# Reordering the opening and the first layer-1 stretch of a one-core attention, Fourier and channel-MLP kernel: pads cleared first, a table's halves on ScalarE, a cast in pieces, and new places for the second weights, batch 2's loads and a small state read

## The chip, the cores and the metric

One core of a Trainium2 chip runs the whole program. The metric is the device time of one execution in microseconds (us), lower is better. "Span" is the profiled part of one execution; it is about 1.8 us shorter than its time.

Engines: PE is TensorE's matmul and PEld its weight load, DVE is VectorE, ACT is ScalarE, POOL is GpSimd, SPq is the queue from which SyncE issues DMA transfers. An execution is called slow if it took over 1.5% longer than the fastest of the same kernel. Ratios and intervals come from fast executions only.

## The reference, cut to what matters

```python
# B, H, S, Ns, D = 8, 8, 512, 32, 64
xread = softmax(x @ state.T / 8) @ state         # 512 rows per batch and head
sread = softmax(state @ x.T / 8) @ x             # 32 rows per batch and head
x = concat(xread, sread) -> (8, 576, 512)        # heads side by side
mixed = real(fft(fft(x, axis=1), axis=2))
u = x + mixed
un = (u - mean) / sqrt(var + 1e-6)               # over the last axis
out = u + relu(un @ w_ch1) @ w_ch2               # 512 -> 2048 -> 512
```

The batches are independent of one another. In each, the scores come first, then the reads, then the Fourier sums, then the two layers.

## The kernel before

The kernel works on one batch at a time, and interleaves small steps of the next batch's attention with the large matmuls of this batch's layers. The Fourier transform is done as matmuls against cosine and sine tables, on sums and differences of mirrored rows. The names that matter below:

- `xs` is a batch's x as loaded (f32), `xin` its bf16 copy (the "cast"), `xT` and `sT` are the transposes of x and state, made by DMA. `esp` are the scores.
- `XF` and `XR` are the reads in forward and reversed row order, `Sm` is a sum of the two, `SS`, `XE`, `XO` and `XQ` are the sums for the transform. Their bf16 low parts (`XEl`, `XQl`) are made by GpSimd and are called "low rows" here.
- `gp` is the transform over rows, `G` its copy, `yp` the transform over columns, made with the second table `TEO`. `U` is u.
- `stb` holds the states as bf16. The state in reversed row order is made by two DMAs: `s_dram<-in_state_dram` writes it to memory, `gen<-s_dram` reads it back.
- `ph` and `po` are layers 1 and 2, with the weights `w1` and `w2` (both `w` in the profile). `warm` are matmuls without a result, put in to keep TensorE's clock up. In the recorded texts `over_s` is the first product of `gp`.

Three places in the opening. The pads are cleared behind the first weights' issue, the halves are on VectorE, and the cast is one instruction:

```python
    def second_halves():
        nc.vector.tensor_scalar(TEO[:, :, 1], in0=TEO[:, :, 0], scalar1=sg, ...)
        nc.vector.tensor_scalar(TEO[0:1, 2], in0=TEO[0:1, 2], scalar1=0.5, ...)
    ...
    for q in range(4):
        nc.gpsimd.dma_start(out=w1[:, :, q * 512:(q + 1) * 512], in_=w1v[...])
    constants()
    clears(0)                # its first two memsets are the pads of XF and XR
    ...
    cast_x(1)
```

And the order of work while batch 0's layer 1 runs (`L[i]` are pieces of that layer, `r1[i]` pieces of batch 1's reads):

```python
    state_blocks(2, 3, nc.gpsimd.tensor_copy)
    turned[2, 0]()           # SyncE: transposes of batch 2's state
    make_mirror()
    nc.gpsimd.tensor_tensor(gate, xs_of[0][:, 0:4], w1[:, :, 3 * 512], op=ALU.add)
    load_x(2)                # SyncE: seven loads of batch 2's x
    turn_in_dram(3, B)       # SyncE: the states of batches 3 to 7, rows reversed
    # [... layer 1 and batch 1's scores ...]
    r1[0](); L[6](); r1[2]()
    load_w2()                # GpSimd: waits for batch 2's x, then issues 4 loads
    r1[1](); L[7](); r1[3](); L[8](); r1[4]()
    cast_x(2)                # GpSimd
    turned[2]()              # SyncE: transposes of batch 2's x
    load_state(3, B, s_dram); load_x(3)
    clear_state(3, B)
```

`load_w2` begins with a one-column copy from `xs` of batch 2, the "gate": it keeps the weights from going ahead of batch 2 in the DMA engines.

The softmax here doesn't subtract the row's maximum and nothing guards it: scores larger than these inputs give would overflow.

## Time and profile before

| | before |
|---|---|
| time, median of 3 | 308.58 us (307.76 to 309.93) |
| span of the profiled execution | 306.6 us |
| TensorE busy | 289.3 us, 94% |
| VectorE, ScalarE, GpSimd busy | 184.4, 135.2, 90.5 us |
| first `yp` of batch 0 | 25.01 us |
| first `gp` of batch 1 | 48.27 us |
| first `yp` of batch 1 | 54.54 us |
| first scores of batch 2 | 57.14 us |

The columns are start, duration, engine, line of the kernel, operation, what it writes from what, shapes, how many in a row, and in brackets how long the engine had waited before it and for whom.

```profile
27.01 2.59 SPq L356 DMA_TRANSPOSE sT<-stb  x2
29.78 5.04 SPq L140 DMA_DIRECT2D xs<-in_x_dram  x7
...
38.66 0.18 POOL L304 COPY gate<-xs 128x4 f32<-128x4 f32 x1
38.79 3.03 POOL L306 DMA_DIRECT2D w<-in_moe_w_ch_dram  x4
...
45.34 6.55 SPq L367 DMA_TRANSPOSE xT<-xin  x4
...
48.27 0.24 PE L754 MATMUL gp<-TC,XQ 128*128 128x144 bf16 x1 [1.90 <-DVE XQ L512]
...
54.54 0.27 PE L659 MATMUL yp<-TEO,G 128*128 128x256 bf16 x1
...
57.14 0.40 PE L411 MATMUL esp<-sT,xT 128*128 128x64 bf16 x8
```

Batch 2's x is asked for at 29.78, behind the transposes. It opens GpSimd's gate, behind the gate stand the weights' issues, the low rows and the cast, behind the cast the transposes of x, and behind those the first scores of batch 2 at 57.14. Nobody waits for that chain: the gate shows no wait.

### The profile page before, as it was taken

How to read it: one execution, taken by the hardware profiler on the slowest of the kernel's cores; microseconds unless marked ns; L12 is line 12 of the kernel's file. 1: busy time of each engine (PE TensorE's matmuls, PEld its weight loads, DVE VectorE, ACT ScalarE, POOL GpSimd, SP SyncE). 2: the span in 40 equal slices, each digit the busy share in tenths (PEclk: the TensorE clock that was granted, in tenths of full speed). 3: DMA queues.
4: the chain of work that ended last, by engine and by line, in shares of the span. 5: the costliest groups of instructions: out<-in, count | busy, mean ns of one | idle time of the engine just before them, and what ended most of it. 6: DMA issues, size and time to landing. Idle time of an engine off the chain costs nothing.

```text
span 306.6 us, 5976 instructions
## 1 busy us (share of the span) xinstructions
PE 289.3 (94%) x2280; PEld 166.3 (54%) x2311; DVE 184.4 (60%) x449; ACT 135.2 (44%) x255; POOL 90.5 (30%) x214
## 2 busy tenths in 40 slices
PE   5697997989999999999999999999999999999996
PEld 4576985545544555456644554445444544555443
DVE  6597689858688485782927756684668484100112
ACT  5566773475653535235452545235523442333300
POOL 5783192483154023600307022701340041000000
PEclk9979997999999999999999999999999999999999
DMA  8992989973942955449252594263343034500346
GB/s 154 203 202 46 177 131 182 184 149 60 188 98 62 191 116 137 90 88 223 50 104 87 109 201 98 58 133 75 82 93 68 34 54 103 116 23 34 68 122 154
DMA packets 110794, 34.86 MB, mean 114 GB/s; under 512 B 101950, under 2 KB 106302, under 8 KB 110766
## 3 DMA queue, kind: packets, MB, share of 16 engines
q1 hardware_dynamic: 100046, 28.72, 46.0%
q0 software_dynamic: 4224, 4.19, 8.5%
q10 hardware_dynamic: 6496, 1.57, 2.5%
q8 instruction: 18, 0.29, 0.4%
q14 instruction: 10, 0.08, 0.1%
HBM read 22.41 MB, written 14.02 MB: 119 GB/s over the span
## 4 chain that ended last, share of the span: by engine, by line
PE 83%; DVE 9%; issue 2%; POOL 2%; DMA 2%; ACT 1%; SPq 0%; DVEq 0%; POOLq 0%; ACTq 0%
PE po L959 36%; PE ph L895 34%; PE gp L754 3%; PE ph L905 2%; DMA xs<-in_x_dram 2%; PE yp L659 1%; PE yp L660 1%; PE po L951 1%; PE xrp L436 1%; POOL w L296 1%; DVE Sm L503 1%; PE xfp L436 1%; PE eTp L423 1%; PE esp L411 1%; DVE TEO L268 1%
## 5 line engine op out<-in xcount | busy, mean ns | idle before, releaser
L959 PE MATMUL po<-w,hT 128*128 128x512 bf16 x478 | 122.5, 381 | 1.6 <-issue 0.9
L897 ACT ACTIVATE hT<-ph 128x512 bf16<-128x512 f32 x112 | 66.8, 597 | 118.3 <-PE ph L895 116.3
L895 PE MATMUL ph<-unT,w 128*128 128x512 bf16 x435 | 112.7, 379 | 0.6
L895 PEld LDWEIGHTS <-w 128*128 128x128 bf16 x576 | 50.6, 98 | 47.4 <-issue 0.8
L959 PEld LDWEIGHTS <-hT 128*128 128x128 bf16 x496 | 47.2, 98 | 46.8 <-issue 0.6
L926 DVE SCALAR_TENSOR_TENSOR ot<-po,rstd,U 128x512 f32<-128x512 f32 (+2 forms) x33 | 24.2, 733 | 51.4 <-PE po L959 49.2
L758 POOL COPY GL<-G 128x128 bf16<-128x128 bf16 x7 | 2.0, 289 | 73.2 <-ACT G L755 73.2
L664 DVE TENSOR_TENSOR U<-yp,XR 128x512 f32<-128x512 f32 x14 | 9.6, 683 | 22.9 <-PE yp L660 22.9
L322 POOL TENSOR_TENSOR rstd<-mv,epst 128x1 f32<-128x1 f32 x34 | 6.6, 194 | 52.0 <-DVE mv L318 52.0
L316 DVE BATCH_NORM_STATS2 st<-U 128x6 f32<-128x512 f32 x32 | 21.7, 679 | 0.0
L323 POOL TENSOR_TENSOR rstd<-rstd,mhalf 128x1 f32<-128x1 f32 x34 | 20.1, 590 | 2.7
L755 ACT CAST G<-gp 128x288 bf16<-128x288 f32 x28 | 13.3, 484 | 8.8 <-PE gp L754 8.8
L905 PE MATMUL ph<-unT,w 128*128 128x128 bf16 x256 | 16.5, 221 | 0.3 <-ACT unT L825 0.3
L143 POOL CAST xin<-xs 128x2048 bf16<-128x2048 f32 (+1 forms) x9 | 14.9, 1660 | 2.5 <-DMA xs<-in_x_dram 2.4
L905 PEld LDWEIGHTS <-w 128*128 128x128 bf16 x256 | 15.2, 99 | 0.7 <-issue 0.6
L813 DVE TENSOR_SCALAR ub<-U,mv 128x512 bf16<-128x512 f32 x24 | 12.3, 512 | 0.9
L991 PE MATMUL warm<-ident 128*128 128x128 bf16 x74 | 8.5, 265 | 3.5 <-POOL xs L285 3.5
L907 ACT ACTIVATE hT<-ph 128x512 bf16<-128x512 f32 x16 | 9.3, 595 | 3.8 <-PE ph L905 3.7
L445 DVE TENSOR_TENSOR XR<-xrp,rs 128x512 bf16<-128x512 f32 x14 | 9.7, 694 | 0.6
L487 POOL COPY XT<-XR 32x514 bf16<-32x514 bf16 x6 | 3.6, 602 | 21.8 <-DVE XR L445 21.7
L445 DVE TENSOR_TENSOR XF<-xfp,rs 128x512 bf16<-128x512 f32 x14 | 9.7, 691 | 0.5
L664 DVE TENSOR_TENSOR U<-yp,XF 128x510 f32<-128x510 f32 x14 | 9.5, 676 | 0.0
(231 smaller groups left out, 377.0 us busy)
## 6 DMA issues: line engine op xcount, KB each, us to landing
xs<-in_x_dram SPq DMA_DIRECT2D x22, 256.0 KB, 3.9
w<-in_moe_w_ch_dram POOLq DMA_DIRECT2D x8, 512.0 KB, 10.4
out_dram<-ot SPq DMA_DIRECT2D x15, 256.0 KB, 3.2
r_dram<-ot SPq DMA_DIRECT2D x14, 256.0 KB, 2.6
out_dram<-r_dram SPq DMA_DIRECT2D x14, 256.0 KB, 3.7
xs<-in_x_dram SPq DMA_DIRECT2D x8, 192.0 KB, 5.0
xs<-in_x_dram ACTq DMA_DIRECT2D x2, 256.0 KB, 5.6
l_dram<-ot SPq DMA_DIRECT2D x2, 256.0 KB, 2.2
```

The lines of the kernel that those rows point to most:

```text
L143: copy(xin_bufs[b % 2][:, lo:hi, 1:513], xs_of[b].rearrange("p (i c) -> p i c", i=4)[:, lo:hi])
L316: nc.vector.bn_stats(st6, u)
L323: nc.gpsimd.tensor_tensor(rstd, rstd, mhalf, op=ALU.pow)
L445: nc.vector.tensor_tensor(ov, in0=p[ps, :, 0:256].rearrange("p g (h d) -> p g h d", d=D), in1=rs[ps].unsqueeze(3).to_broadcast([n, 2, 4, D ...
L664: nc.vector.tensor_add(u.rearrange("p (k r) -> p k r", r=2), p.rearrange("p (r k) -> p k r", r=2)[:, 0:u.shape[1] // 2, :], x.rearrange("p ...
L755: nc.scalar.copy(G[:, j, :].rearrange("p (i q) -> p q i", q=2), p[:, 0:NM].rearrange("p (q i) -> p q i", q=2))
L813: nc.vector.tensor_scalar(t, in0=ud, scalar1=mv[:, 0:1], scalar2=None, op0=ALU.subtract)
L895: nc.tensor.matmul(ph[:, o:o + n], lhsT=w1[:, c, f * 128:(f + 1) * 128], rhs=un_of[key][:, c, :], start=(c == 0), stop=(c == DC - 1))
L897: nc.scalar.activation(hT[:, per * i:per * i + per, :].rearrange("p a b -> p (a b)"), ph, AF.Relu, scale=-1.0 / 512 if key == 0 else -1.0 ...
L905: nc.tensor.matmul(ph[:, o:o + 128], lhsT=w1[:, c, f * 128:(f + 1) * 128], rhs=un_of[key][:, c, 128 * r:128 * r + 128], start=(c == 0), st ...
L926: nc.vector.scalar_tensor_tensor(ot[:, cols], in0=po_of[i][:, 0:cols.stop - cols.start], scalar=rstd, in1=u[:, cols], op0=ALU.mult, op1=AL ...
L959: nc.tensor.matmul(po_of[i], lhsT=h_of[key][:, f, i * 128:(i + 1) * 128], rhs=w2[:, f, :], start=(f == 0), stop=(f == FC - 1))
```

## The change

Its intent: take three stalls out of the way (VectorE waiting for the pads; VectorE held up beside GpSimd's cast of batch 1; the same beside the cast of batch 2). The diff, cut to its core:

```diff
     def second_halves():
-        nc.vector.tensor_scalar(TEO[:, :, 1], in0=TEO[:, :, 0], scalar1=sg, scalar2=None, op0=ALU.mult)
-        nc.vector.tensor_scalar(TEO[0:1, 2], in0=TEO[0:1, 2], scalar1=0.5, scalar2=None, op0=ALU.mult)
+        nc.scalar.activation(TEO[:, :, 1], TEO[:, :, 0], AF.Copy, scale=sg)
+        nc.scalar.mul(TEO[0:1, 2], TEO[0:1, 2], 0.5)
 # [...]
     nc.gpsimd.memset(xs_of[1][0:1, 0:1], 0.0)
+    clear_pads(0)
+    clear_pads(1)
 # [...]
+    constants()
+    clears(0)
     for q in range(4):
         nc.gpsimd.dma_start(out=w1[:, :, q * 512:(q + 1) * 512], in_=w1v[:, :, q * 512:(q + 1) * 512])
-    constants()
-    clears(0)
 # [... sread of batches 0 and 1 becomes sread_heads: one product per head into
 #      XQ, and state_rows: four transposing matmuls and one copy into XR ...]
-    cast_x(1)
+    for i in range(4):
+        cast_x(1, lo=i, hi=i + 1)
 # [... second_halves() moves up, behind second_sines(); the warm(10) that stood there becomes warm(6) ...]
-    turned[2, 0]()
     make_mirror()
     nc.gpsimd.tensor_tensor(gate, xs_of[0][:, 0:4], w1[:, :, 3 * 512], op=ALU.add)
     load_x(2)
+    turned[2, 0]()
     turn_in_dram(3, B)
 # [...]
     L[6]()
+    load_w2(0, 2)
     r1[2]()
-    load_w2()
     r1[1]()
-    L[7]()
-    r1[3]()
-    L[8]()
-    r1[4]()
     cast_x(2)
     turned[2]()
     load_state(3, B, s_dram)
     load_x(3)
-    clear_state(3, B)
+    load_w2(2, 4)
+    L[7]()
+    r1[3]()
+    r1[6]()
+    L[8]()
+    r1[4]()
 # [...]
+    clear_state(3, B)
```

`load_w2(lo, hi)` issues the quarters lo to hi - 1 and has the gate only where lo is 0; `r1[6]` is `state_rows`. I call the hunks of the pads, the first weights' issue, the halves (with four warming matmuls fewer) and the cast in pieces the opening, and the rest the tail.

More of the change, by code (lines that the diff above doesn't have):

```diff
@@ L267, in second_halves, with clear_pads, clears @@
     def second_halves():
-        nc.vector.tensor_scalar(TEO[:, :, 1], in0=TEO[:, :, 0], scalar1=sg, scalar2=None, op0=ALU.mult)
-        nc.vector.tensor_scalar(TEO[0:1, 2], in0=TEO[0:1, 2], scalar1=0.5, scalar2=None, op0=ALU.mult)
+        nc.scalar.activation(TEO[:, :, 1], TEO[:, :, 0], AF.Copy, scale=sg)
+        nc.scalar.mul(TEO[0:1, 2], TEO[0:1, 2], 0.5)
     def exp_again():
         nc.scalar.activation(gate2[:, 3:4], gate2[:, 0:1], AF.Exp)
-    def clears(i):
+    def clear_pads(i):
         nc.gpsimd.memset(XFs[i][:, :, 512:514], 0.0)
         nc.gpsimd.memset(XRs[i][:, :, 0:514:513], 0.0)
+    def clears(i):
         if i == 0:
@@ L294, with load_w2 @@
         cast_x(0, lo=i, hi=i + 1)
+    constants()
+    clears(0)
     for q in range(4):
         nc.gpsimd.dma_start(out=w1[:, :, q * 512:(q + 1) * 512], in_=w1v[:, :, q * 512:(q + 1) * 512])
-    constants()
-    clears(0)
     def clear_state(lo, hi):
         nc.gpsimd.memset(stb[:, lo:hi].rearrange("p b g c -> p (b g c)").bitcast(F32), 0.0)
-    def load_w2():
-        nc.gpsimd.tensor_copy(gate, xs_of[2][:, 0:2048:512])
-        for q in range(4):
+    def load_w2(lo, hi):
+        if lo == 0:
+            nc.gpsimd.tensor_copy(gate, xs_of[2][:, 0:2048:512])
+        for q in range(lo, hi):
             nc.gpsimd.dma_start(out=w2[:, q * 4:(q + 1) * 4, :], in_=w2v[:, q * 4:(q + 1) * 4, :])
@@ L447, in xread @@
                 in1=rs[ps].unsqueeze(3).to_broadcast([n, 2, 4, D]), op=ALU.mult)
-        def sread():
-            rcs = wk.tile([128, 2], F32, name="rcs", tag="rcs")
-            for g in range(2):
-                p = qt("srp")
-                for si in range(4):
-                    nc.tensor.matmul(p[:, 0:257], lhsT=E[:, si, g, :], rhs=xin[:, si, 257 * g:257 * g + 257],
-                                     start=(si == 0), stop=(si == 3))
-                nc.vector.reciprocal(rcs[:, g:g + 1], p[:, 256 * g:256 * g + 1])
-                for hh in range(4):
-                    c0 = 512 - (256 * g + 64 * hh)
-                    ph = slice(32 * hh, 32 * hh + 32)
-                    o = XR[0:32, 0, c0:c0 - 64:-1]
-                    i = p[ph, 1 - g + 64 * hh:65 - g + 64 * hh]
-                    if g == 0 and b > 0:
-                        nc.vector.tensor_scalar(o, in0=i, scalar1=rcs[ph, g:g + 1], scalar2=None, op0=ALU.mult)
-                    else:
-                        nc.scalar.activation(o, i, AF.Copy, scale=rcs[ph, g:g + 1])
         def sread_by_head():
@@ L483, in sread_by_head, with sread_heads, state_rows @@
                                         in1=rcs[ph].unsqueeze(2).to_broadcast([32, 2, D]), op=ALU.mult)
+        def sread_heads():
+            p = qt("srp")
+            for g in range(2):
+                for si in range(4):
+                    for hh in range(4):
+                        c0 = 1 + 256 * g + 64 * hh
+                        nc.tensor.matmul(p[32 * hh:32 * hh + 32, 64 * g:64 * g + 64], lhsT=E[:, si, g, 32 * hh:32 * hh + 32],
+                                         rhs=xin[:, si, c0:c0 + 64], start=(si == 0), stop=(si == 3))
+            for g in range(2):
+                for si in range(4):
+                    nc.tensor.matmul(p[:, 128 + g:129 + g], lhsT=E[:, si, g, :], rhs=xin[:, si, 0:1], start=(si == 0), stop=(si == 3))
+            rcs = wk.tile([128, 2], F32, name="rcs", tag="rcs")
+            nc.vector.reciprocal(rcs, p[:, 128:130])
+            nc.vector.tensor_tensor(XQ[:, 0:2 * D].rearrange("p (g d) -> p g d", g=2),
+                                    in0=p[:, 0:128].rearrange("p (g d) -> p g d", g=2),
+                                    in1=rcs.unsqueeze(2).to_broadcast([128, 2, D]), op=ALU.mult)
+        def state_rows():
+            p = qt("hdp")
+            pv = p[0:32, :].rearrange("p (h g d) -> p h g d", h=4, g=2)
+            for hh in range(4):
+                nc.tensor.matmul(pv[:, hh], lhsT=ident[:, 32 * hh:32 * hh + 32], rhs=XQ[:, 0:2 * D].rearrange("p (g d) -> p g d", g=2),
+                                 start=True, stop=True)
+            nc.scalar.copy(XR[0:32, 0, 512:0:-1].rearrange("p (g h d) -> p h g d", g=2, d=D), pv)
         def read_low():
@@ L534, in attend @@
         if b < 2:
-            second = [read_low, sread, fold_low, read(0, False, XF[:, 0, 0:512]),
+            second = [read_low, sread_heads, fold_low, read(0, False, XF[:, 0, 0:512]),
                       lambda: (fold_rows(slice(0, 1)), fold_low_again()),
-                      read(128, False, XF[:, 1, 0:512]), None,
+                      read(128, False, XF[:, 1, 0:512]), state_rows,
                       lambda: (read(256, True, XR[:, 1, 1:513])(), fold())]
@@ L1042 @@
     second_sines()
-    warm(10)
+    second_halves()
+    warm(6)
     even(1)
@@ L1057 @@
     terms_of(2, 0)
-    second_halves()
     out_of(1)
```

## The prediction

> **What bounds the kernel now.** I read the page's slices first, then the waits of the first 50 us, the order of work around each long wait, and the chain that ended last. From the page (40 slices of 7.7 us, busy tenths; PEclk is the granted TensorE clock):
>
> ```profile
> PE   5697997989999999999999999999999999999996
> PEclk9979997999999999999999999999999999999999
> ```
>
> From slice 9 on TensorE is full: cut into stretches, it is busy 9.95 of 10 us in 70:80 and 49.58 of 50 in 200:250. What comes after about 60 us is TensorE work that the change leaves as it is. So a microsecond is worth something only where it lets that stretch begin earlier, and I looked for what delays it. The waits in 0:50 (who, for whom: total us, times, longest):
>
> ```profile
> POOL XEl L490 <- DVE XT L487: 9.6, 1, 9.6
> ...
> DVE XR L604 <- POOL XR L276: 3.1, 1, 3.1
> ...
> PE gp L754 <- DVE XQ L512: 1.9, 1, 1.9
> ...
> PE yp L659 <- DVE G L736: 1.6, 1, 1.6
> ```
>
> GpSimd's 9.6 us is idleness of an engine that nobody waits for there. The other three are on the path, and the order of work shows what is behind each (start us, us, engine, instruction). First, VectorE's first normalisation waits 3.12 us for the clearing of a pad, which stands in GpSimd's queue behind four issues of the first weights:
>
> ```profile
> 9.03 3.20 POOL L296 DMA_DIRECT2D w<-in_moe_w_ch_dram  x4
> ...
> 12.35 0.16 POOL L276 MEMSET XR<- 128x4 bf16 x1
> ...
> 12.54 0.69 DVE L604 TENSOR_TENSOR XR<-xrp,rs 128x512 bf16<-128x512 f32 x1 [3.12 <-POOL XR L276]
> ```
>
> Second, the table's halves on VectorE take 2.59 us beside GpSimd's cast of batch 1, and the copies of G, for which TensorE waits, stand behind them:
>
> ```profile
> 21.20 1.89 POOL L143 CAST xin<-xs 128x2048 bf16<-128x2048 f32 x1
> 21.22 2.59 DVE L268 TENSOR_SCALAR TEO<-TEO,sg 128x512 bf16<-128x512 bf16 x1
> ...
> 23.98 0.88 DVE L736 CAST G<-gp 128x288 bf16<-128x288 f32 x3
> ```
>
> Third, the same with batch 2's cast and the row sum Sm, which takes 0.43 us at 40.17 and 2.70 here:
>
> ```profile
> 42.90 2.70 DVE L503 TENSOR_TENSOR Sm<-XF,XR 128x514 bf16<-128x514 bf16 x1
> 43.40 1.91 POOL L143 CAST xin<-xs 128x2048 bf16<-128x2048 f32 x1
> ```
>
> The chain runs through all of these, and through VectorE, ScalarE and small TensorE steps between 35.9 and 48.2 us; in 28.2 to 35.7 and after about 60 it is TensorE alone.
>
> **What the Trainium skill says.** "SBUF — State Buffer", § Who interferes with whom: VectorE and GpSimd share one pair of ports under an exclusive lock; a tensor_scalar in a two-port mode contends with GpSimd, a tensor_tensor with two SBUF inputs contends with a GpSimd instruction that reads SBUF, and one with at most one SBUF input outside these modes does not. The trace agrees: 2.59 and 2.70 us above, while normalisations out of PSUM keep 0.69 to 0.70 us beside any GpSimd work. "DMA: Bandwidth & Descriptors", § SWDGE vs HWDGE vs iDMA: a DMA from GpSimd has its descriptors computed there; the four issues held GpSimd 3.20 us. "ScalarE: Activation LUTs", § Table sets: copy is in every set, so the halves on ScalarE need no table load; a trace duration for such work is the 0.72 us of a 128x512 activation with a pointer (TEO at 20.23). "TensorE: Matmul & The Clock Gate", § What's actually happening: the clock falls to half after an idle window of some 3.4 us. The trace: after the idle of 46.4 to 48.3 a 128x512 matmul takes 631 ns where 379 is usual, until 52.4; after the idle of 1.6 us at 23.4 there was no such drop.
>
> **The change, part by part (times of the new kernel are estimates from the durations above).**
>
> *Pads first.* Four clears at a pitch of 0.035 us go ahead of GpSimd's casts, where it waited 2.42 us for a DMA anyway. The normalisation starts at 9.45 instead of 12.54. Next in line is the fourth score: it needed VectorE's reciprocal (13.48 + 0.20) and now finds it at about 11.0, but needs ScalarE's copy of x, which ended at 11.40. So it starts at 11.45, not 13.74: 2.3 of the 3.1 us come through. VectorE's normalisations and even/odd sums up to 21.29 follow at that distance. The remaining clears (some 0.8 us) now go ahead of the weights' issue: 9.9 to 13.1; GpSimd's low rows, which started at 15.91, can start at 13.45.
>
> *Halves to ScalarE.* VectorE loses 2.59 + 0.21 us. ScalarE gains about 0.7 + 0.35 after the sines (about 17.2 to 18.2), before its first copy of G (21.67 - 2.3 = 19.3): hidden. The last copies of G then wait for TensorE's last term, which ended at about 22.95, now 20.65; two copies of 0.27 bring 21.2, TensorE goes on at 21.35 where it was 25.01. Shift so far 3.65, of which this part has 1.35: not 2.8, since the terms end behind VectorE anyway. The cast in four pieces (about 18.8 to 21.8; pieces took 0.84 alone) meets only copies out of PSUM, and ends before the transposes of batch 1 (25.88 - 3.65 = 22.2).
>
> *First weights.* They landed at 16.8, 20.2, 22.8 and 25.4; now up to 0.8 later. Layer 1 would start at 24.3 and read a further quarter each 1.3 us, the last at some 28.3: no wait. Batch 2's load waits for the last quarter: about 26.1 instead of 29.78, as two transposes of 2.59 us no longer precede it.
>
> *State read by head.* 32 + 8 + 4 small matmuls (0.46 + 0.29 + 0.22 us of issue) replace 8 of 257 columns (0.86): even. The path from 37.27 to 40.15 (two reciprocals, four multiplies of VectorE, four of ScalarE, 0.28 to 0.32 each) becomes reciprocal, one multiply of 0.29, transposing matmuls and a copy of 0.60, which meet normalisations needed anyway: 0.6 us gained on the path to the first row sum.
>
> *Second weights in two pairs.* GpSimd now waits for batch 2 (26.1 + 8.3, as before from 29.78 to 38.1: 34.4), issues two (1.55), does the low rows (1.4), and casts at about 37.5 to 39.4. The second Sm comes to about 38.8: 0.6 us are still lost there instead of 2.27. Behind it XQl (four of 0.45) may press on XE and XQ: up to 0.5.
>
> *Sum.* From 35.9 on: 3.65 + 0.6 + 2.27 - 0.6 - 0.3 = 5.6 us at the first XQ (48.2 to about 42.6). TensorE has layer-1 work until about 42.1, so its idle time falls from 1.9 to about 0.5 us and I expect the clock to hold: over_s, layer 1 and the first layer-2 products ran some 4 us at about half rate and lost about 1.8. Of that only the 0.89 us that VectorE waits at 55.18 for yp passes on; beyond it VectorE's four statistics (51.0 to 54.3) and the sums of U set the pace. 5.6 + about 0.7 = 6.3, less an allowance of 0.4 for small waits in the new order: 5.9 us. 308.6 - 5.9 = 302.7.
>
> **Rivals.** (1) The lock moves rather than goes: the cast covers the second Sm whole, or GpSimd's low rows hold XE and XQ as three successive GpSimd instructions held Sm at 42.9. For it: the cast is still only 1 us from Sm by my times. Against: batch 2 would have to land later than 35. It makes the shift 4.2 to 4.5, the clock drops again, and the time 304.2. (2) Weights become the bound: the first ones later and needed 3.65 us sooner, or the third and fourth quarter of the second, issued at about 39.5 to 41. They took 5.7 to 13.2 us to land; needed at about 49.5 and 52. For: the queues are full then; against: less traffic stands before them. It costs 1 to 2 us: 304.5. (3) All stalls add up: 3.1 + 2.8 + 2.3 + 0.6, and the clock 1.8. This asks that nothing else is as late, and the fourth score and the last terms are. It would give 299. (4) Hidden altogether, as TensorE is 94% busy: against it, the stalls lie before 60 us and end on the chain, where TensorE's busy time is partly warming matmuls.
>
> **Range and chances.** The uncertain sizes are the contention in 38 to 43 (about 1 us each way), the clock (0.7) and the landing of weights (up to 1.5 one way). I take 300.9 to 304.9. Two per cent is 6.2 us, a little more than I expect: faster by over 2% 0.42, within 2% 0.57, slower 0.01.
>
> **What would show it.** Right: no wait of VectorE for the pads, and the fourth score at about 11.5 behind ScalarE's copy; TEO halves on ScalarE under 0.8 us; first yp at 21.4, layer 1 at 24.3; Sm under 1.2 us; first XQ at about 42.6; no 631 ns matmuls near 44 to 48; from 60 on the same TensorE work, some 6 us earlier. Wrong: layer 1 waiting for w, GpSimd's second gate later than 35.5, Sm or XE near 2 us, po waiting for w2, or a gap of TensorE over 1.5 us with a low clock at about 40 to 46.

## The result, and the profile after

| | before | after |
|---|---|---|
| median of the predicted job | 308.57 us (307.76 to 309.93) | 301.25 us (300.73 to 306.59) |
| ratio of fast runs | 1 | 0.9756, interval 0.9719 to 0.9793 |

A ratio is the mean time of one kernel's fast runs over that of the other's of the same rounds, so it is not quite the ratio of the medians. The change is 7.3 us faster in the median of this job. In two further jobs (after_again and after_five below) the ratio was 0.9821 and 0.9813, with intervals that reach 0.9893 and 0.9854; so the gain is clear, and whether it is over 2% is not.

The four executions after were 306.59, 301.2, 301.3 and 300.73. The first is slow, and it is the one with the profile. A fifth, outside this median, took 301.49. I ran the same kernel in two more jobs, and both times the profiled execution was slow again (307.2 and 308.46). So no profile of a fast execution of exactly this kernel exists. Up to 43 us the three profiles agree closely (the first `gp` of batch 1 starts at 42.92 in this one, at 42.77 and 42.69 in the others), and I read them there. For what follows I use a variant that differs in one place and whose profile is a fast one (`four_first`, below).

The page's slices of after, the rows that answer to those shown in the prediction:

```profile
PE   5989895799999999999999999999999999999996
...
PEclk9999999999999999999999999999999999999999
```

TensorE's clock is never below 90% in a slice. Before, slices 3 and 7 had a 7 there (15.3 to 23.0 us and 46.0 to 53.7 us, at 7.66 us a slice). The 5 and 7 in slices 7 and 8 of the row PE are gaps of this slow execution between 46 and 61 us.

The waits of after in 0:60 (who, for whom: total us, times, longest):

```profile
PE po L969 <- DMA w<-in_moe_w_ch_dram: 3.6, 2, 2.2
...
POOL gate L308 <- DMA xs<-in_x_dram: 2.7, 1, 2.7
...
PE esp L415 <- DMA xT<-xin: 1.7, 2, 1.2
...
PE xrp L440 <- DVE XF L449: 1.5, 1, 1.5
...
PE esp L590 <- ACT xT L578: 0.6, 1, 0.6
```

Gone are VectorE's 3.1 us for the pads, TensorE's 1.9 for `XQ` and 1.6 for `G`. New are GpSimd's wait for batch 2's x at the gate, and TensorE's waits for the second weights (`po`) and for batch 2's transposes (`esp`). For this kernel the last two are known from slow executions only, since no other was profiled. TensorE waits for `xT` in fast executions of variants too (1.5 us in four_again, 0.2 in four_first).

The timeline of after, opening:

```profile
9.47 0.69 DVE L614 TENSOR_TENSOR XR<-xrp,rs 128x512 bf16<-128x512 f32 x1
...
9.74 3.33 POOL L302 DMA_DIRECT2D w<-in_moe_w_ch_dram  x4
...
17.13 0.72 ACT L268 ACTIVATE TEO<-TEO,sg 128x512 bf16<-128x512 bf16 x1
...
18.77 2.29 POOL L143 CAST xin<-xs 128x512 bf16<-128x512 f32 x4
...
20.68 0.27 PE L669 MATMUL yp<-TEO,G 128*128 128x256 bf16 x1 [0.27 <-DVE G L746]
```

The first normalisation starts at 9.47 without a wait (before: 12.54). The table's half costs ScalarE 0.72 us where it cost VectorE 2.59. `yp` of batch 0 starts at 20.68, which is 4.33 us earlier.

The timeline of after, from there to batch 2's first scores:

```profile
22.22 7.18 SPq L140 DMA_DIRECT2D xs<-in_x_dram  x7
29.51 2.68 SPq L360 DMA_TRANSPOSE sT<-stb  x2
...
31.80 0.19 POOL L308 COPY gate<-xs 128x4 f32<-128x4 f32 x1 [2.68 <-DMA xs<-in_x_dram]
...
35.13 1.90 POOL L143 CAST xin<-xs 128x2048 bf16<-128x2048 f32 x1
...
35.32 2.01 DVE L513 TENSOR_TENSOR Sm<-XF,XR 128x514 bf16<-128x514 bf16 x1
...
37.06 15.56 SPq L371 DMA_TRANSPOSE xT<-xin  x4
...
39.63 0.49 DVE L513 TENSOR_TENSOR Sm<-XF,XR 128x514 bf16<-128x514 bf16 x1
...
42.92 0.23 PE L764 MATMUL gp<-TC,XQ 128*128 128x144 bf16 x1
...
55.41 0.29 PE L415 MATMUL esp<-sT,xT 128*128 128x64 bf16 x4 [1.18 <-DMA xT<-xin]
```

Batch 2's x is now asked for at 22.22, 7.56 us earlier, and its transposes of state come behind it. The cast runs at 35.13, beside the first `Sm` (2.01 us; 1.75 and 1.17 in the other two profiles) and no longer beside the second (0.49). `gp` of batch 1 starts 5.35 us earlier and without a wait. The transposes of `xT` take 15.56 us to issue where they took 6.55. Between `gp` and batch 2's first scores TensorE waits 3.6 us for the second weights and 1.2 us for `xT`, and the first scores come only 1.7 us earlier in this execution.

### The profile page after: what moved, and what is told of

Its sections match the earlier page's. It is cut to its first block, busy times and chain, and to the rows that moved or that the text cites. A ratio compares the mean times of both kernels' runs of the same rounds, so it can differ in the third digit from the quotient of the medians.

```text
span 304.8 us, 6036 instructions
## 1 busy us (share of the span) xinstructions
PE 286.5 (94%) x2312; PEld 164.0 (54%) x2343; DVE 181.0 (59%) x443; ACT 135.6 (44%) x254; POOL 91.3 (30%) x217
## 4 chain that ended last, share of the span: by engine, by line
PE 78%; DMA 11%; SPq 4%; POOL 3%; issue 1%; DVE 1%; ACT 1%; ACTq 0%; POOLq 0%; DVEq 0%
PE po L969 35%; PE ph L905 34%; DMA xT<-xin 5%; SPq L140 3%; DMA s_dram<-in_state_dram 3%; DMA xs<-in_x_dram 3%; PE gp L764 2%; PE po L961 1%; PE yp L669 1%; PE yp L670 1%; POOL w L310 1%; PE xfp L440 1%; PE xrp L440 1%; PE esp L415 1%; PE eTp L427 1%
## 5 line engine op out<-in xcount | busy, mean ns | idle before, releaser
L143 POOL CAST xin<-xs 128x512 bf16<-128x512 f32 (+1 forms) x12 | 15.1, 1280 | 2.5 <-DMA xs<-in_x_dram 2.4
L1001 PE MATMUL warm<-ident 128*128 128x128 bf16 x70 | 7.4, 249 | 3.5 <-POOL xs L287 3.5
L420 ACT ACTIVATE E<-esp 128x512 bf16<-128x512 f32 x14 | 8.4, 599 | 2.6 <-PE esp L415 2.6
```

What stands on the lines that cost most here:

```text
L143: copy(xin_bufs[b % 2][:, lo:hi, 1:513], xs_of[b].rearrange("p (i c) -> p i c", i=4)[:, lo:hi])
```

## The experiments

All twelve runs gave correct results. The first four shared one job and its seven runs of before (median 308.7 us), the next four another (median 307.89), the last four a third with eleven runs (median 309.1).

| label | times, us | ratio to before, interval |
|---|---|---|
| after_again (slow: 307.2) | 307.2, 302.04, 301.82, 306.05 | 0.9821 (0.9748 to 0.9893) |
| opening_only | 310.74, 307.01, 309.45, 307.84 | 0.9976 (0.9933 to 1.0019) |
| tail_only | 305.3, 304.48, 305.34, 306.42 | 0.9888 (0.9858 to 0.9919) |
| pads_only | 309.09, 308.89, 307.81, 306.76 | 0.9977 (0.994 to 1.0015) |
| x2_late | 306.33, 307.16, 308.08, 307.42 | 0.9971 (0.9927 to 1.0015) |
| four_first | 301.06, 301.51, 302.53, 301.69 | 0.9791 (0.9748 to 0.9833) |
| state_late | 305.2, 301.71, 302.58, 302.19, 303.55 | 0.9805 (0.9758 to 0.9853) |
| old_sread | 307.57, 303.88, 303.26, 306.91 | 0.9911 (0.9836 to 0.9985) |
| opening_x2 | 303.54, 303.6, 303.5, 304.12, 304.43 | 0.9842 (0.9815 to 0.9868) |
| after_five (slow: 308.46, 306.69) | 308.46, 306.69, 305.42, 302.18, 302.07, 302.4 | 0.9813 (0.9771 to 0.9854) |
| four_again | 303.22, 303.67, 302.04, 302.27, 302.63 | 0.9805 (0.9778 to 0.9831) |
| four_state | 301.31, 305.02, 301.38, 304.81, 302.52, 303.25 | 0.9814 (0.9773 to 0.9854) |

### 1. The changed kernel again: after_again

No edit.

> The changed kernel once more, for a profile in the fast state. Theory A (the last stretch of the gain is the clock and the idle time of 46.4 to 48.3 us in the kernel before): in a fast run the first over_s matmul is at 42.9 as in the slow profile, TensorE then goes on to the first yp without waiting over 0.5 us for w2 or xT, with no matmul at half rate, and the span is near 299.4. Theory B (waits for w2 and for the transposes of x are there in fast runs too, only shorter): po waits for w by 1 us or more in all, and the time is still 301.2.

Two executions near 301.9 and two at 306 to 307. The profiled one, a slow one, shows TensorE waiting 3.0 us for the second weights. The ratio is therefore less sure than the first job's, and with no fast profile neither theory is decided.

### 2. The opening alone: opening_only

```diff
 # the kernel before, with the opening's hunks and nothing of the tail
+    clear_pads(0); clear_pads(1)            # and clears(0) ahead of w1's issue
+    # halves on ScalarE, behind second_sines(); cast_x(1) in four pieces; warm(10) -> warm(6)
     turned[2, 0]()
     make_mirror()
     load_x(2)
```

> The kernel before with the opening's parts alone: pads first, weights' issue after the clears, halves on ScalarE, cast of batch 1 in four pieces. If the parts add up: the first yp at 20.7 instead of 25.0, 4.3 us gained, 304.3; idle time and half-rate clock near 42 to 48 stay as in the kernel before. Rival: if the later wait for the first sum of XQ takes part of it back, under 3 us are gained, 305.6 or more.

Nothing of the opening's gain is left that is clear of noise: 0.9976, with an interval that holds 1. Its timeline:

```profile
26.95 1.28 POOL L163 CAST stb<-gen 32x128 bf16<-32x128 f32 x4 [4.34 <-DMA gen<-s_dram]
...
28.25 3.71 SPq L360 DMA_TRANSPOSE sT<-stb  x2
32.14 5.07 SPq L140 DMA_DIRECT2D xs<-in_x_dram  x7
...
40.55 0.40 POOL L308 COPY gate<-xs 128x4 f32<-128x4 f32 x1 [5.69 <-DMA xs<-in_x_dram]
...
44.03 0.59 POOL L501 TENSOR_TENSOR XQl<-XEl 32x128 bf16<-32x128 f32 x1
...
44.67 0.24 PE L758 MATMUL gp<-TC,XQl 128*128 128x144 bf16 x1 [2.01 <-POOL XQl L501]
...
57.23 0.77 PE L415 MATMUL esp<-sT,xT 128*128 128x64 bf16 x8 [2.89 <-DMA xT<-xin]
```

Batch 1 is ahead: its `yp` is at 51.58 (before 54.54). But batch 2's x is loaded at 32.14, later than before. The transposes ahead of it in SyncE's queue start as soon as GpSimd has cast batch 2's state, and these casts wait 4.34 us for the transfer of the reversed state. It was issued at 21.56, against 21.70 before, since SyncE waits about 9 us for `s_dram<-in_state_dram` in both kernels. In before, pads_only and x2_late too the transposes start within 0.03 us of the casts' end (at 27.01, 28.07 and 26.66). So the load stands behind a chain that the opening does not move. GpSimd waits 5.69 us at the gate for it, so the weights' issue, the low rows and the cast are late. First TensorE waits 2.01 us for `XQl`, then 2.89 us for `xT`, and batch 2's first scores start at 57.23 where before they started at 57.14. The chain that nobody waited for has become the one that ends last.

### 3. The tail alone: tail_only

```diff
 # the changed kernel, with the opening's hunks taken back
-    clear_pads(0); clear_pads(1)
-    for i in range(4):
-        cast_x(1, lo=i, hi=i + 1)
+    cast_x(1)
 # and second_halves() back on VectorE behind terms_of(2, 0), warm(6) back to warm(10),
# w1's issue back ahead of clears(0)
```

> The kernel before with the other parts alone: read by head, second weights in two pairs around batch 2's cast, batch 2's load ahead of its transposes. If the parts add up: 7.3 - 4.3 = 3.0 us gained, 305.6, of which 1.0 us is there at the first over_s matmul and the rest comes from the idle time and the half-rate matmuls that are gone. Rival: without the earlier opening the x of batch 2 is in time and the first row sum meets the cast in the same way; then under 1.5 us are gained, 307.1 or more.

0.9888, 3.4 us. The gate opens at 31.32, `gp` starts at 46.47 (1.80 earlier than before), no half-rate clock follows, and batch 2's first scores start at 53.68. The tail gains by itself what it was made for, at the second `Sm`.

### 4. The pads alone: pads_only

```diff
+    clear_pads(0); clear_pads(1)            # and clears(0) ahead of w1's issue
```

> The kernel before with the pads first and the weights' issue after the clears, nothing else. If what limits is the fourth score behind ScalarE's copy: 2.4 us at the normalisations and at the first yp, 306.1. Rival: if the halves on VectorE beside the cast take longer when both come earlier, under 1.5 us, 307 or more; if the clock's fall at 15 to 17.5 us cost more than I think, 3.0 us, 305.6.

0.9977. `yp` of batch 0 comes 2.5 us earlier (22.51), as expected, but the earlier start ends in a longer wait: the trace has TensorE waiting 4.1 us for `XQ` before `gp`, which starts at 47.94 (before: 1.9 us of wait, 48.27).

```profile
38.91 0.19 POOL L308 COPY gate<-xs 128x4 f32<-128x4 f32 x1 [2.77 <-DMA xs<-in_x_dram]
...
42.82 4.60 DVE L515 COPY XE<-SS 128x2 f32<-128x2 f32 x1
```

GpSimd waits for batch 2's x here too. Its low rows and cast run from 42.38 to 46.25, and a two-column copy of VectorE, ahead of `XQ`, takes 4.60 us beside these and the memset behind them (to 47.39), where it took 0.16 before. A stall removed some 35 us ahead of that place only moved the idle time.

### 5. The changed kernel with batch 2's x behind its state's transposes: x2_late

```diff
-    load_x(2)
     turned[2, 0]()
+    load_x(2)
     turn_in_dram(3, B)
```

> The changed kernel with batch 2's load behind its two transposes again, as in the kernel before; nothing else undone. Theory A (the opening's gain passes on only because batch 2's x lands at 31.8 us instead of about 40, and with it everything of GpSimd that stands behind the gate): first yp still at 20.7, but the gate is passed near 39 to 40, the low rows near 41, the first over_s matmul near 46 and the time is 305 to 307.5. Theory B (the load's place is a detail; the cast and the reads bring the gain): first over_s at 43 to 44, time 301 to 303.

0.9971 (the interval holds 1): the swap of two adjacent lines takes back all of the change that is clear of noise. In its timeline the gate waits, and a sum of VectorE is held up:

```profile
38.25 0.44 POOL L308 COPY gate<-xs 128x4 f32<-128x4 f32 x1 [10.82 <-DMA xs<-in_x_dram]
...
40.01 4.02 DVE L520 TENSOR_TENSOR XE<-SS 128x512 f32<-128x512 f32 x1
```

The gate waits 10.82 us. GpSimd's low rows (40.25 to 41.6) and cast (41.58 to 43.48) come together with `XE`, which takes 4.02 us where it takes 0.70 in the changed kernel. `gp` starts at 44.70 after a wait of 3.02, the clock is at 0.52 and 0.62 of full speed in 44:48 and 48:52, and batch 2's scores start at 55.31.

### 6. Four weight loads together: four_first

```diff
-    load_w2(0, 2)
+    load_w2(0, 4)
 # [...]
-    load_w2(2, 4)
```

> The changed kernel with all four quarters of the second weights issued together where the first two are now. Theory A (in the runs of 305 to 307 us the later quarters, issued at 37 to 38.5 us just as the transposes of x begin, land late): po no longer waits 3 us for w, and all four runs lie within 1.5 us of each other at 301 to 302.5. Theory B (sharing between the weights and the transposes as such makes the slow runs, whoever is issued first): two kinds of runs again, some over 304. In either case GpSimd's low rows and the cast come 1.5 us later, so the first row sum (2.01 us beside the cast) takes under 1 us.

301.06 to 302.53, no slow execution, as theory A had it, and the profile is a fast one:

```profile
38.05 7.75 SPq L371 DMA_TRANSPOSE xT<-xin  x4
...
42.15 0.24 PE L764 MATMUL gp<-TC,XQ 128*128 128x144 bf16 x1
...
46.76 0.27 PE L669 MATMUL yp<-TEO,G 128*128 128x256 bf16 x1
...
49.36 0.28 PE L415 MATMUL esp<-sT,xT 128*128 128x64 bf16 x4
...
49.88 0.29 PE L415 MATMUL esp<-sT,xT 128*128 128x64 bf16 x4 [0.23 <-DMA xT<-xin]
```

`gp` is 6.12 us earlier than in the kernel before, `yp` and batch 2's scores 7.8, the end of the span 7.3 (299.3 against 306.6). TensorE waits for no weight.

### 7. The states' turning later: state_late

```diff
     turned[2, 0]()
-    turn_in_dram(3, B)
 # [...]
     turned[2]()
+    turn_in_dram(3, B)
     load_state(3, B, s_dram)
```

> The changed kernel with the copy of the remaining states (DRAM to DRAM, 256-byte packets) issued behind the transposes of batch 2's x instead of ahead of them. Theory A (the transposes stand behind this copy on the same queue, which is slowed by the weights): the four transposes take 6 to 7 us of issue instead of 15, esp waits for xT by under 0.3 us, and no run is over 303. Theory B (it is the weights and the transposes themselves): transposes still 13 us or more in a run over 304.

In between: the transposes' issue takes 8.56 us and there is no wait for weights, and four of five executions are at 301.7 to 303.6; the profiled one is at 305.2. Theory A's other two signs failed: two executions are over 303, and TensorE waits 0.7 us for `xT`. The profiled one lost its time later than anything above: TensorE was busy 8.54 us of 10 in 70:80, with the clock at 0.83 there.

### 8. Batch 1's old read of the state: old_sread

```diff
-            second = [read_low, sread_heads, fold_low, ...
-                      read(128, False, XF[:, 1, 0:512]), state_rows,
+            second = [read_low, sread, fold_low, ...
+                      read(128, False, XF[:, 1, 0:512]), None,
```

> The changed kernel with batch 1's state read as in the kernel before (8 matmuls of 257 columns, four multiplies of VectorE, four of ScalarE). Prediction's step (0.6 us on the path): 0.6 us slower than the changed kernel. Theory B (the first row sum then comes at about 37, behind the cast, so what the read costs the contention gives back): within 0.5 us of it. Fast runs 301.0 to 302.5 either way.

303.26 and 303.88 in the better executions, where the changed kernel has 300.7 to 302.4 in its better ones of three jobs and four_first, in this job, a mean of 301.7. By the times the read by head would be worth 1.5 to 2 us, not 0.6; but this rests on two executions, and the profile does not bear it out: the first `gp` starts at 43.05, only 0.1 to 0.4 us later than in the three profiles of the changed kernel. The size stays open. Two executions at 307 have the waits of the changed kernel's slow ones (the transposes' issue took 14.91 us in the profiled one), so the ratio mixes two things.

### 9. The opening and the order of batch 2's loads, nothing else: opening_x2

```diff
 # opening_only, with one line moved
-    turned[2, 0]()
     make_mirror()
     nc.gpsimd.tensor_tensor(gate, xs_of[0][:, 0:4], w1[:, :, 3 * 512], op=ALU.add)
     load_x(2)
+    turned[2, 0]()
```

> The kernel before with the opening of the change (pads first, halves on ScalarE, cast in pieces) and only one thing from its second half: batch 2's x is loaded ahead of the transposes of its state. Theory (the opening's 4 us were lost, in the opening alone, to batch 2 landing late, which put its gate, the second weights' issue, low rows and cast of GpSimd into the row sums): the gate falls to about 32 us instead of 40.6, the first over_s product to 43 to 44.5, and the time to about 303.5 to 305. Rival (the rest of the second half, weights in pairs round the cast and the read by head, is what carries the gain): over_s after 46.5, time 306.5 or more.

303.5 to 304.43, ratio 0.9842, and the narrowest spread of all: 4.9 us with an opening that alone gave nothing. This is the counterpart of x2_late; together they show that the order of these two lines decides whether the opening's gain reaches the end. The swap alone, on the kernel before, was not run. tail_only, which contains it, gained 3.4 us, so the times do not tell how much of the 4.9 us the swap would bring by itself; `gp` comes 2.5 us earlier here than in tail_only (43.95 against 46.47).

```profile
21.97 6.38 SPq L140 DMA_DIRECT2D xs<-in_x_dram  x7
28.45 3.20 SPq L360 DMA_TRANSPOSE sT<-stb  x2
...
34.36 0.18 POOL L308 COPY gate<-xs 128x4 f32<-128x4 f32 x1
...
38.69 2.61 DVE L507 TENSOR_TENSOR Sm<-XF,XR 128x514 bf16<-128x514 bf16 x1
...
43.95 0.24 PE L758 MATMUL gp<-TC,XQ 128*128 128x144 bf16 x1 [1.80 <-DVE XQ L516]
...
51.17 0.40 PE L415 MATMUL esp<-sT,xT 128*128 128x64 bf16 x8
```

The gate passes without a wait, behind the low rows' first part. Time and `gp` are as expected; for the gate I had expected about 32 us, and it is 34.36 because GpSimd did not get to it sooner. The second `Sm` still takes 2.61 us beside the cast, and `gp` comes 1.8 us later than in four_first, after a wait of 1.80. four_first, which has the rest of the tail, shows neither.

### 10. Five rounds: after_five, four_again, four_state

The first is the changed kernel without an edit, the second is the kernel of four_first.

> The changed kernel once more, in five rounds, beside the version with its four weight loads together. Theory (its executions come in two kinds, and the later kind is one in which the second weights and batch 3's transposes share the DMA engines and TensorE waits for the weights): some executions at 301 to 302.5 and some at 305 to 307, the mean ratio 0.978 to 0.982. Rival (the slow ones were the chip's and not the kernel's): all within 1.5 us, ratio 0.975 to 0.977.

The changed kernel again had two kinds of executions: 302.07 to 302.4, and 305.42 to 308.46. Of its 14 executions in three jobs six are over 305, with a mean of 303.9 over all. (The 1.5% rule counts 305.42 and, in after_again, 306.05 as fast. Without these the better executions have a ratio of about 0.978 in both jobs, worked out from the means.)

> The four weight loads of layer 2 together, ahead of the cast, as in four_first. Theory (loads issued before batch 3's transposes do not share their engines with them, at no cost to the path): 301 to 302.5 in every execution, mean lower than the changed kernel's of this job by 1 us or more, and no wait of po for w. Rival (pairs are needed to keep GpSimd's issue out of the row sums): 1 us slower than the changed kernel's better executions.

302.04 to 303.67, a little above the expected 301 to 302.5, and TensorE waits for no weight. Over both jobs the nine executions of this version lie between 301.06 and 303.67, with a mean of 302.3. So it is steadier than the changed kernel, 1.6 us better in the mean over all executions, and not faster than the changed kernel's better executions (0.9805 against 0.9813 in the fast runs of this job). The rival, that it would be 1 us slower than those, did not hold: it is 0.5 us slower in the mean of this job.

```diff
 # four_state
-    load_w2(0, 2)
+    load_w2(0, 4)
-    turn_in_dram(3, B)                      # behind turned[2, 0]()
+    turn_in_dram(3, B)                      # behind turned[2]()
-    load_w2(2, 4)
```

> Four weight loads together and also the turning of batch 3 to B's x in memory moved behind the state's transposes (as in state_late). If what is left of the wait is the transposes' share of the DMA engines: no slower than four_again, 300.5 to 302. If the later transposes are themselves needed by batch 3's rows: 1 us or more slower than four_again.

Two of six executions were near 305. The later turning does not help, and may hurt. Rows of the table by stretches (stretch, its length, then busy us and number of instructions of PE, PEld, DVE, ACT, POOL, then granted clock, DMA share, GB/s), state_late first:

```profile
70.00:80.00 10.00, 8.54 (x57) 4.98 (x59) 3.12 (x8) 4.43 (x8) 0.85 (x3) 0.83 0.86 171
```

and four_state in an execution of 301.31 us:

```profile
70.00:80.00 10.00, 10.00 (x70) 5.55 (x69) 6.66 (x17) 6.69 (x15) 1.97 (x6) 1.00 0.79 160
```

With the same order of the turning, one execution has the gap and the other has not. Which transfers meet which in the DMA engines differs from execution to execution here.

### One number that goes with all profiles

Taken together, the profiles show where the end of the program is decided. The table has the start of batch 2's first scores (of their second half, where they are split by a wait), the span, and the difference. Profiles of executions called slow are left out.

| profile | first scores of batch 2 | span | rest |
|---|---|---|---|
| before | 57.14 | 306.6 | 249.5 |
| pads_only | 56.81 | 307.3 | 250.5 |
| opening_only | 57.23 | 309.0 | 251.8 |
| x2_late | 55.74 | 304.6 | 248.9 |
| tail_only | 53.68 | 303.5 | 249.8 |
| opening_x2 | 51.17 | 301.8 | 250.6 |
| four_again | 51.97 | 301.4 | 249.4 |
| four_first | 49.88 | 299.3 | 249.4 |
| four_state | 49.35 | 299.5 | 250.2 |
| old_sread | 55.74 | 305.8 | 250.1 |
| state_late | 50.23 | 303.4 | 253.2 |

Ten of the eleven rests lie within 3 us of each other while the first column moves by 8; the eleventh is the execution with the gap at 70:80. From soon after batch 2's first scores TensorE is nearly full in all of these (8.96 to 9.95 us of 10 in 60:70), and the program is the same. The three slow profiles of the changed kernel fit too: first scores at 56.26, 54.85 and 56.93, rests of 248.5, 250.6 and 249.8. So they lose their time ahead of batch 2's scores, where TensorE waits for `w` and `xT`, and not later.

## Why the prediction was right or wrong

The size and direction held: 301.25 us measured, 302.7 predicted, within the range. My chance for "faster by over 2%" was 0.42; the first job came out there, the two later ones just short of it. Two of my signs of being wrong came as well: an `Sm` of 2.01 us, and `po` waiting for `w2` in the slow profiles. Step by step:

- **Pads first: right, a little more came through.** No wait for the pads, and the fourth score waited 0.6 us for ScalarE's copy, as worked out; it started at 11.31 (predicted 11.45). The last read of batch 0 came 2.43 us earlier (13.61 against 16.04), against 2.3 predicted.
- **Halves to ScalarE: right in kind, 0.7 us too small.** 0.72 and 0.41 us on ScalarE, hidden. The first `yp` came at 20.68, not 21.35. The term that was mis-sized is the last term of the transform, which came 2.97 us earlier and not 2.3: TensorE's clock was at 0.83 of full speed in 10:20 before and at 1.00 after, which I had not counted here. (pads_only keeps all the warming matmuls and has that term at the same 19.56 us as the changed kernel, so the four fewer are not the reason.)
- **First weights: wrong about batch 2's load, and this is the step that failed.** I had the load wait for the last quarter and start at about 26.1, and took its earlier start for a by-product of the order, worth the 2.59 us of the transposes' issue. It started at 22.22, right behind the issue of the reversed state's transfer (21.57) and 6.70 us before the instruction that reads the last quarter (`gate<-xs,w`, 28.92). What it was freed from is the wait of the transposes for GpSimd's casts of the state (opening_only shows it), and its place ahead of them is what the whole shift rests on: opening_only against opening_x2 (0.9976 and 0.9842), and x2_late against the changed kernel (0.9971, and 0.9756 to 0.9821 in its three jobs). The working names no condition under which the opening's 3.65 us would reach the end, and there is one: batch 2 has to come earlier too, and in the old order the opening does not bring it forward.
- **State read by head: size not settled.** Predicted 0.6 us; old_sread has 0.1 to 0.4 us at `gp`, and 1.5 to 2 us in its two better executions.
- **Second weights in two pairs: the contention moved to another row sum.** GpSimd's gate came at 31.80 and not at 34.4, so the cast ran at 35.1 and not at 37.5, and met the first `Sm` (2.01 us) and not the end of the second (0.49). The first `gp` was predicted at 42.6 and came at 42.92. Two errors nearly cancel there, so that this time came out is partly luck: the cast fell on the first `Sm`, which leaves TensorE waiting 1.5 us for `XF`, and the opening gave 0.7 us more. And the pairs are not needed: four_first keeps the four together and is as fast.
- **The sum: mis-sized at the clock.** Of the 1.8 us that the low clock had cost, I passed on about 0.7, of 0.89 at most, holding that VectorE's statistics would set the pace. In four_first the stretch from `gp` to `yp` took 4.61 us, before 6.27: 1.66 of the 1.8 came through. (tail_only and opening_x2, whose clock held as well, have 4.61 and 4.62; pads_only, whose clock fell to 0.57, has 6.28.) With 6.12 at `gp` this makes 7.78 at `yp`, and 7.3 at the end.
- **Rivals.** Rival 1 (the lock moves rather than goes) was right about the movement and wrong about the cost. Rival 2 (weights become the bound) happened in the profiled, slow executions: TensorE waited 3.6, 3.0 and 3.8 us for the second weights. Rivals 3 and 4 fell for the whole; but the opening alone is hidden altogether, as rival 4 has it, for a reason that I had not named.

What stays open is why the changed kernel has two kinds of executions. A lower clock is not all of it: the mean granted clock was 1.000 in the profiled execution of 306.59 us. In its slow profiles the transposes of `xT` take 12.65 to 15.56 us to issue, in four_first and four_again 7.75 and 10.68. The weights' second pair is issued at 36.97, together with the transposes at 37.06; in tail_only the two fall together as well, at 40.54 and 40.62, and there the issue takes 6.22. So it is not the pair alone, and four_state has late executions without any pair. No profile of a fast execution of the changed kernel exists to compare with.

## What to carry to other kernels

Before removing a stall, look for the second chain that runs beside the one with the stall, and ask how far ahead it is: here the next batch's load was just early enough for the old pace, and two stalls removed gave nothing until that load was put ahead of two transposes. Ask also what the instruction ahead of it in its queue waits for: here what counted was not its 2.59 us of issue but a transfer two steps back. When the parts of a change are measured one at a time, a part that gives nothing alone may carry most of the gain together with another, so try a part both alone and left out. A single early event whose distance to the end hardly varies, such as the first scores of batch 2 here (within 3 us in all but one profile of the table), tells more quickly than any list of waits whether a gain will reach the end.

## What the Trainium skill lacked or had wrong

- "SBUF — State Buffer", § Who interferes with whom, says that whoever issues first has the shared ports for its whole instruction and the other blocks. The runs agree for one instruction (2.01 us of `Sm` beside a cast of 1.90), but the page does not say that the loser can stay blocked through several GpSimd instructions in a row: `XE` took 4.02 us in x2_late, from 40.01 on, through the low rows that began at 40.25 and the cast that ended at 43.48. By the recorded starts `XE` was first, by 0.24 us, and was held all the same.
- "DMA: Bandwidth & Descriptors", § Queues, rings and completion order, says that each DMA engine goes round its queues packet by packet. That makes sharing between weights and transposes likely. The page has a bandwidth for transposes, but not what they cost beside other transfers: the same four took from 6.07 us (pads_only) to 15.56 us (after) to issue. By which transfers, the runs do not show.
- "TensorE: Matmul & The Clock Gate", § What's actually happening, puts the fall of the clock after an idle window of about 3.4 us. In the kernel before, TensorE's longest named wait near 46 us was 1.9 us, and the clock was at 0.64 of full speed in 48:52; in opening_x2 a wait of 1.80 us at the same step left it at 1.00. So a wait of under 2 us can come with the drop or without it, and the page's idle window, longer than either wait, does not tell which; that the page calls the window free-running says where it may begin, not that a shorter idle stretch suffices. TensorE was busy 2.37 us of 4 in 44:48 before, and 2.19 us of 4 in 40:44 in opening_x2, so the busy share does not tell it either.
